# A planner's clock gets a duration for each kind of operation, and a bank's addition gets a due time

## The chip, the cores and the metric

The kernel runs on one core of one Trainium2 chip. The metric is the device time of one execution in microseconds (us). The engines are TensorE (PE, with its weight loads as PEld), VectorE (DVE), ScalarE (ACT), GpSimd (POOL) and SyncE (SP, which issues most DMAs).

## The reference

Three layers follow each other on 16384 tokens of 192 channels. The weights of the convolution are a softmax over its 7 taps, one set for each of 8 groups of channels.

```python
out = einsum('hk,bskhg->bshg', softmax(weight), windows_of_7(x))   # causal, per sequence of 4096
h = out @ w_in1;  g = relu(h) ** 2;            x2 = g @ w_out1     # 192 -> 2048 -> 192
h = x2 @ w_in2;   g = maximum(0.01 * h, h);    y  = g @ w_out2     # 192 -> 2048 -> 192
```

## The kernel before

The tokens are cut into 32 tiles of 512 (`TT`). For each tile and layer the 2048 hidden columns are done in 8 steps of 256 (two chunks of 128), which makes 512 steps `s` (`steps`). The first 64 steps do tiles 0 to 3 in both layers (tiles 0 and 1 as a pair that shares its weights). From step 64 on a round of 32 steps does two tiles: 8 steps each for layer 1, then 8 each for layer 2. There are 14 rounds, and during 13 of them DVE prepares the next two tiles. Numbers are kept as a high and a low part in fp32r, so each product is made of several matmuls. Two matmuls of 64 rows run side by side in the two halves of the array.

In each step PE makes `h` of step s (`g1`, `h` in the profile, psum tiles with 4 buffers) and, in three groups between the h products, the second product of step s-2 (`g2_one`, into three of the four banks o0m, o1m, o0r, o1r). ACT evaluates h (`act`, lines 567 and 569), makes the high parts `hi` (line 594) and in layer 1 the square of one chunk (line 576). DVE makes the other square (line 574, layer 1), the low parts `lo` (line 598) and their sum `both` (line 610), which PE needs two steps later. This order of a step on ACT and DVE is `chain` in `single`.

When a tile's 8 steps are done (the steps with s mod 8 = 1, called leaving steps here), its three banks are emptied by `evac_one`: ACT copies bank E (line 733, "e") and half of F (line 736, "f"), DVE adds F and E (line 739, "z", the bank's addition), and in the next step M (lines 742 and 743). The new product in the next bank can't start before line 739 has read it. What is left then lies in queues of pieces: `leave` (split of layer 1's result into the next operand x at lines 466 and 475, or for layer 2 the transpose to the output tile y at lines 753 and 758, followed by 4 stores each on SP at line 787), `prep` (the convolution of the next tiles on DVE: transposes at line 402, first tap at line 424, six more taps at line 426 for each of three passes, then the split into x, whose copies between partitions go by DMA at line 444) and `dec` (weights). The output tile y has one buffer: the next pair's transposes wait for the stores of the last one. The first pair of layer 2 is emptied by `evac` with transposes at lines 847 and 852 and 12 stores.

From step 48 (`THREE`) on, `single` plans DVE and ACT with a small clock of its own in ns, `clock`: before each DVE operation of the chain, `fill` puts pieces from the queues as long as `ends`, a trial run of the rest of the chain, stays within the due time `by`; a piece that is not due yet may delay it by 40 at most. A piece is a tuple with its step and its cost first; the convolution's pieces come from this line of `conv`:

```python
return acc, [((750 if k else 490), lambda k=k: tap(k)) for k in range(K)]
```

so 490 stands for the first tap and 750 for the later ones; transposes have 700, low parts of the split 690 and lines 742 and 743 together 1300.

Of the kernel before, what the change touches and what calls it, by code (L numbers as in the profile page):

```python
# [18 lines left out]
P = 128  # L19
TT = 512  # L20
STEP = 4100
PAIR = 215.6
STEP_ = 18 * PAIR
ON_A, ON_D, LATENCY = 545, 615, 70
DEBT = -4000
LAG = 2
AHEAD = 2
# [4 lines left out]
COVER = 2  # L32
# [33 lines left out]
def conv_moe_moe2_kernel(  # L66
# [11 lines left out]
    B, S, D = x.shape  # L78
# [252 lines left out]
    own = const.tile([P, 2, H], F32, name="own")  # L331
# [56 lines left out]
    at, end = slice(HALO - K + 1, HALO), slice(HT - K + 1, HT)  # L388
# [113 lines left out]
    now, made = [0], {}  # L502
# [38 lines left out]
    hps, gsp, hi, lo, ops = {}, {}, {}, {}, {}  # L541
# [21 lines left out]
    def act(u, f):  # L563

        g = gsp[u, f] = pg.tile([P, TT], F32, tag="g", name="g")
        if u[0] == 1:
            nc.scalar.activation(out=g, in_=hps.pop((u, f)), func=ACTF.Relu)  # L567
        else:
            nc.scalar.activation(out=g, in_=hps.pop((u, f)), func=ACTF.Prelu, alpha=0.01)  # L569

    def square(u, f, vector):
        g = gsp[u, f]
        if vector:
            nc.vector.tensor_mul(out=g, in0=g, in1=g)  # L574
        else:
            nc.scalar.activation(out=g, in_=g, func=ACTF.Square)  # L576
# [12 lines left out]
    def high(u, f, dma=False):  # L589
        a = hi[u, f] = spare_tile() if late_chunk(u, f) else ph.tile([P, TT], F32R, tag="hi", name="hi")  # L590
        if dma:
            nc.gpsimd.dma_start(out=a, in_=gsp[u, f])
        else:
            nc.scalar.copy(out=a, in_=gsp[u, f])  # L594

    def low(u, f):
        b = lo[u, f] = spare_tile() if late_chunk(u, f) else pl.tile([P, TT], F32R, tag="lo", name="lo")
        nc.vector.tensor_sub(out=b, in0=gsp.pop((u, f)), in1=f32(hi[u, f]))  # L598
# [104 lines left out]
    def turns_of(p):  # L703
        return ((0, 1, 2), (1, 2, 0)) if p % 2 == 0 else ((2, 1, 0), (0, 2, 1))
# [153 lines left out]
    with tc.manual_schedule():  # L858
# [77 lines left out]
        def decode_one():  # L936
            cost, fn = dec.popleft()[1:3]
            fn()
            budget[0] -= cost
            return cost  # L940
# [5 lines left out]
        prep, leave = deque(), deque()  # L946
# [70 lines left out]
        first = (1, 0)  # L1017
# [51 lines left out]
        chain = {"A": [deque() for _ in range(4)], "Z": [deque() for _ in range(4)]}  # L1069
# [49 lines left out]
        def needed(s, n):  # L1119

            while n > 0 and dec and dec[0][4] <= s:
                n -= decode_one()
            return n
# [19 lines left out]

        clock = {"D": 0, "A": 0}

        def on(engine, took, after=0):
            clock[engine] = max(clock[engine], after) + took
            return clock[engine] + LATENCY

        def ends(chain, extra, at):  # L1150

            now_, done = dict(clock), {}
            now_["D"] += extra
            for name, engine, took, needs in chain:
                start = max([now_[engine]] + [done.get(n, at.get(n, 0)) for n in needs])
                now_[engine] = start + took
                done[name] = now_[engine] + LATENCY
            return now_["D"]

        def fill(s, chain, at, by, scalar=0):  # L1160

            while True:
                best = None
                for q in (leave, prep, dec):
                    if not q or (q[0][3] and not q[0][3]()):
                        continue
                    cost = q[0][1]
                    if cost < 0 and not scalar:
                        continue
                    if cost > 0:  # L1170
                        end = ends(chain, cost, at)
                        if end > (by if q[0][0] <= s else min(by, ends(chain, 0, at) + 40)):
                            continue
                    if best is None or q[0][0] < best[0][0]:
                        best = q
                if best is None:
                    return
                if best is dec:
                    decode_one()
                    continue  # L1180
                z = best.popleft()
                z[2]()
                if z[1] < 0:
                    scalar -= 1
                    on("A", -z[1])
                else:
                    on("D", z[1])

        def single(s, begun, A, Z, leaving, then, alone):

            l, u = A[0][0], A[0]
            p = A[1] // 2
            at = {"h": begun + 5 * PAIR + 2 * (3 + COVER) * PAIR + 300}
            first = min(j for order in turns_of(p) for j, k in enumerate(order) if k == (1 if (u[1] % 2 == 0) else 2))
            by = begun + 2 * STEP_ + (5 + 3 * first + COVER * first + 2) * PAIR - 250
            names = ("actZ", "actA") if l == 1 else ("actA", "actZ")
            chain = [(names[0], "A", ON_A, ("h",)), (names[1], "A", ON_A, ("h",))]
            if l == 1:
                chain += [("sqZ", "D", ON_D, ("actZ",)), ("sqA", "A", ON_A, ())]
            chain += [("hiA", "A", ON_A, ("actA",)), ("hiZ", "A", ON_A, ("sqZ", "actZ"))]  # L1200
            chain += [("loA", "D", ON_D, ("hiA",)), ("loZ", "D", ON_D, ("hiZ",)), ("c", "D", ON_D, ("loZ",))]
            do = {
                "actA": lambda: act(*A), "actZ": lambda: act(*Z), "sqZ": lambda: square(*Z, True), "sqA": lambda: square(*A, False),
                "hiA": lambda: high(*A), "hiZ": lambda: high(*Z), "loA": lambda: low(*A), "loZ": lambda: low(*Z),
                "c": lambda: add_low(u, p),
            }
            if alone:
                early, other, add_rest = leaving
                at["E"], at["F"] = begun + STEP_ - 3 * PAIR + 300, begun + STEP_ + 300
                chain = [("e", "A", ON_A, ("E",)), chain[0], ("f", "A", ON_A, ("F",)), ("z", "D", ON_D, ("F", "e"))] + chain[1:]  # L1210
                do.update(e=early, f=other, z=add_rest)
            elif leaving:
                for fn in leaving:
                    fn()
                at["F"] = begun + STEP_ + 300
                chain = [("e", "A", ON_A, ("F",)), ("e2", "D", ON_D, ("F",)), ("s", "A", 2 * ON_A, ("F",)), ("z", "D", 2 * ON_D, ("s",))] + chain
            while chain:
                name, engine, took, needs = chain[0]
                if engine == "D":
                    fill(s, chain, at, by, 1 if name == "loA" else 0)  # L1220
                if name in do:
                    do[name]()
                at[name] = on(engine, took, max([at.get(n, 0) for n in needs] + [0]))
                chain = chain[1:]
            if alone:
                leave.append((s, 1300, then[0], None, None))
                then = then[1:]
            return then

        prep_next = 2  # L1230
        begun = 0
# [3 lines left out]
        for s in range(NS):  # L1235
            u, p = steps[s]
            l, t = u
            leaving, alone = [], False
            u2, p2 = steps[s - LAG] if s >= LAG else (None, 0)
            if s == NS - 1:  # L1240
                advance(going)
            elif s < LAG or u2 in in_pair:
# [4 lines left out]
                if s >= LAG:  # L1247
                    f = 2 * p2 + u2[1] % 2
# [3 lines left out]
                    z = g2(pair, f)  # L1252
# [3 lines left out]
                    if f == NF - 1:  # L1256
                        leaving, then = evac(pair)
                going = follows
            else:
                z = g2_one(u2, p2)  # L1260
# [6 lines left out]
                if p2 == NP - 1:  # L1267
                    alone = True
                    leaving, then = evac_one(u2)
# [6 lines left out]
            A, Z = (u, 2 * p), (u, 2 * p + 1)  # L1276
# [16 lines left out]
            if leaving:  # L1293
                while leave:
                    z = leave.popleft()
# [9 lines left out]
            if three:  # L1305
                begun += STEP_
                if s == THREE:
                    clock["D"] = clock["A"] = begun
                if late:
                    if late[0] not in hi:  # L1310
                        high(*late[0])
                    low(*late.pop())
                needed(s, 10000)
                then = single(s, begun, A, Z, leaving, then if leaving else (), alone)
                release()
                if leaving:
                    own = (2, u2[1]) if u2[0] == 1 else None
                    wait = LEAVE if u2[0] == 1 else LEAVE + 2
                    leave.extend((s + wait + 0.5 * n, c, fn, gate, own) for n, (c, fn, gate, own) in enumerate(
                        [z if len(z) == 4 else z + (None,) for z in then]  # L1320
                    ))
                continue
# [34 lines left out]
            if alone:  # L1357
                then[0]()
                then = then[1:]
# [3 lines left out]
            if leaving:  # L1363
                own = (2, u2[1]) if u2[0] == 1 else None
# [38 lines left out]
```

## Time and profile before

| | |
|---|---|
| median of 3 runs | 2066.9 us (2065.8 to 2067.23) |
| the profiled execution | 2066.62 us, its span 2064.9 us, granted clock 0.998 |
| PE busy | 2050.2 us, 99% of the span |
| DVE busy | 1697.2 us, 82% |
| ACT busy | 1465.3 us, 71% |
| line 598 (lo) on DVE | 1022 times, mean 690 ns |
| line 610 (both) on DVE | 463 times, mean 692 ns |
| line 426 (later taps) on DVE | 174 for acc_a, mean 746 ns |
| line 424 (first tap) on DVE | 29 for acc_a, mean 483 ns |

The span runs from the first to the last instruction of the profiled execution. An engine that is busy nearly all the time sets the end, so the places to look for are those where it waits, and for whom. In a timeline a row has start, duration, engine, line, operation, output and input, a count where equal ones follow each other, and in brackets the engine's idle time ahead of it and what ended it.

### The profile page before, as it was taken

Reading aid. Unit: us, or ns where it says so; the run is one execution under the profiler, and the core shown is the slowest. Engines: PE = TensorE matmul, PEld = TensorE weight load, DVE = VectorE, ACT = ScalarE, POOL = GpSimd, SP = SyncE. Lnnn points to the kernel's source line nnn. Section 1 sums busy time; section 2 is a strip of 40 time slices with the busy share of each in tenths; the row PEclk is TensorE's granted clock in tenths of the full one; section 3 lists DMA queues with packets and bytes.
Section 4 is the critical chain, followed back from the end, with each engine's and each line's share of the span. In section 5 each row is a group of like instructions: output and inputs, shape, how many; then the busy total and the mean of one; then the engine's idle time right before and its main releaser. Section 6 shows DMA issues by size and latency. Waiting matters only on the chain.

```text
span 2064.9 us, 46890 instructions
## 1 busy us (share of the span) xinstructions
PE 2050.2 (99%) x18592; PEld 1974.7 (96%) x18592; DVE 1697.2 (82%) x2651; ACT 1465.3 (71%) x2651; POOL 30.9 (1%) x82
## 2 busy tenths in 40 slices
PE   9999999999999999999999999999999999999998
PEld 6999999999999999999999999999999999999997
DVE  8988878888887887879878788887878878788674
ACT  7887667677676776767677676776767667676774
POOL 1000210000000000000000000000000000000000
PEclk9999999999999999999999999999999999999999
DMA  8631131121212112131121211212122121311110
GB/s 188 159 98 37 24 60 27 41 38 47 39 25 57 32 42 37 31 59 27 38 39 41 45 27 41 38 47 38 25 52 33 46 36 28 62 27 38 23 34 17
DMA packets 233397, 95.24 MB, mean 46 GB/s; under 512 B 203928, under 2 KB 219416, under 8 KB 233176
## 3 DMA queue, kind: packets, MB, share of 16 engines
q1 hardware_dynamic: 230008, 89.06, 21.9%
q0 software_dynamic: 1168, 2.75, 0.7%
q8 instruction: 145, 2.38, 0.5%
q14 instruction: 76, 0.62, 0.1%
q10 hardware_dynamic: 2000, 0.42, 0.1%
HBM read 25.19 MB, written 12.58 MB: 18 GB/s over the span
## 4 chain that ended last, share of the span: by engine, by line
PE 92%; DVE 3%; ACT 2%; DMA 1%; SPq 1%; issue 1%; DVEq 0%; ACTq 0%
PE h L535 45%; PE o1m L535 16%; PE o0r L535 15%; PE o0m L535 8%; PE o1r L535 8%; ACT hi L594 1%; DVE lo L598 1%; DMA lent<-in_moe_w_out_dram 0%; DMA out_dram<-y 0%; DVE acc_a L426 0%; DVE acc_b L426 0%; SPq L787 0%; ACT g L567 0%; DVE g L574 0%; DVE x L475 0%
## 5 line engine op out<-in xcount | busy, mean ns | idle before, releaser
L535 PE MATMUL h<-x,w 64*128 64x512 f32 x9216 | 1349.5, 376 | 0.9 <-ACT g L569 0.5
L535 PEld LDWEIGHTS h<-x,w 64*128 64x128 f32 x9216 | 1063.2, 186 | 8.5 <-ACT g L569 0.9
L598 DVE TENSOR_TENSOR lo<-g,hi 128x512 fp32r<-128x512 f32 x1022 | 668.4, 690 | 296.5 <-ACT hi L594 282.0
L594 ACT CAST hi<-g 128x512 fp32r<-128x512 f32 x1020 | 590.0, 620 | 62.6 <-DVE g L574 51.7
L535 PE MATMUL o1m<-hi,w 64*128 64x512 f32 x2044 | 621.5, 381 | 1.0 <-DVE ring L739 0.8
L535 PE MATMUL o0r<-hi,w 64*128 64x512 f32 x1948 | 589.5, 380 | 0.4 <-DVE ring L739 0.3
L569 ACT ACTIVATE g<-h 128x512 f32<-128x512 f32 x512 | 282.9, 595 | 316.0 <-PE h L535 315.2
L535 PE MATMUL o0r<-lo,w 64*128 64x512 f32 (+1 forms) x1022 | 382.1, 376 | 0.0
L535 PEld LDWEIGHTS o1m<-hi,w 64*128 64x128 f32 x2044 | 357.7, 185 | 25.5 <-DVE ring L739 3.3
L567 ACT ACTIVATE g<-h 128x512 f32<-128x512 f32 x512 | 281.9, 594 | 133.1 <-PE h L535 130.8
L535 PEld LDWEIGHTS o0r<-hi,w 64*128 64x128 f32 x1948 | 342.9, 185 | 21.6 <-DVE ring L739 3.5
L535 PE MATMUL o1m<-both,w 64*128 64x512 f32 x926 | 348.5, 376 | 2.5 <-DVE both L610 2.5
L610 DVE TENSOR_TENSOR both<-lo 128x512 fp32r<-128x512 f32 x463 | 320.5, 692 | 18.4 <-PE h L535 0.5
L535 PE MATMUL o0m<-hi,w 64*128 64x512 f32 x1088 | 324.5, 378 | 0.0
L535 PE MATMUL o1r<-hi,w 64*128 64x512 f32 x1052 | 318.7, 378 | 0.0
L535 PE MATMUL o0m<-lo,w 64*128 64x512 f32 x560 | 208.2, 376 | 0.6 <-DVE lo L598 0.6
L535 PE MATMUL o1r<-lo,w 64*128 64x512 f32 (+1 forms) x526 | 197.9, 376 | 0.0
L535 PEld LDWEIGHTS o0m<-hi,w 64*128 64x128 f32 x1088 | 191.9, 186 | 1.2
L535 PEld LDWEIGHTS o0r<-lo,w 64*128 64x128 f32 (+1 forms) x1022 | 186.7, 183 | 0.5
L535 PEld LDWEIGHTS o1r<-hi,w 64*128 64x128 f32 x1052 | 186.1, 186 | 1.0
L535 PEld LDWEIGHTS o1m<-both,w 64*128 64x128 f32 x926 | 172.2, 186 | 4.1 <-DVE both L610 3.4
L576 ACT ACTIVATE g<-g 128x512 f32<-128x512 f32 x269 | 169.5, 633 | 7.9
(134 smaller groups left out, 1315.8 us busy)
## 6 DMA issues: line engine op xcount, KB each, us to landing
x<-x SPq DMA_DIRECT2D x189, 256.0 KB
out_dram<-y SPq DMA_DIRECT2D x186, 64.0 KB
raw_a<-in_x_dram SPq DMA_DIRECT2D x127, 64.0 KB
raw_b<-in_x_dram SPq DMA_DIRECT2D x62, 64.0 KB
lent<-in_moe_w_out_dram SPq DMA_DIRECT2D x13, 256.0 KB
lent<-in_moe_w_in_dram SPq DMA_DIRECT2D x13, 192.0 KB
lent<-in_moe_w_in_dram SPq DMA_DIRECT2D x13, 128.0 KB
lent<-in_moe_w_out_dram SPq DMA_DIRECT2D x13, 128.0 KB
```

The costliest lines, as they stand in the source:

```text
L535: return nc.tensor.matmul(out=o.rearrange("p (b a) -> p b a", a=2), lhsT=w, rhs=z.rearrange("p (a b) -> p b a", a=2), start=begin, stop=end_,)
L567: nc.scalar.activation(out=g, in_=hps.pop((u, f)), func=ACTF.Relu)
L569: nc.scalar.activation(out=g, in_=hps.pop((u, f)), func=ACTF.Prelu, alpha=0.01)
L576: nc.scalar.activation(out=g, in_=g, func=ACTF.Square)
L594: nc.scalar.copy(out=a, in_=gsp[u, f])
L598: nc.vector.tensor_sub(out=b, in0=gsp.pop((u, f)), in1=f32(hi[u, f]))
L610: nc.vector.tensor_add(out=c, in0=f32(lo[u, 2 * p]), in1=f32(lo[u, 2 * p + 1]))
```

## The change

The step `PAIR` of PE goes from 215.6 to 216 ns, one duration for ACT and one for DVE becomes a table by kind of operation (`TOOK`), pieces get planned durations by their tag (`PIECE`), the delay until another engine sees a result becomes one for each engine, and `by` has a due time for the bank's addition `z` beside that for `both` (`c`). A piece is put only if neither of the two comes later than its due time (a piece not due yet: than 40 more). Output transposes of layer 2 get a gate: not before step s + 5 of the leaving step s.

```diff
-PAIR = 215.6
+PAIR = 216
-ON_A, ON_D, LATENCY = 545, 615, 70
+TOOK = {"act": 500, "sqA": 525, "hi": 525, "e": 485, "f": 485, "sqZ": 612, "lo": 612, "c": 612, "z": 710}
+PIECE = {750: 420, 490: 668, 700: 660, 690: 610, 1300: 1325}
+AFTER_PE, AFTER_A, AFTER_D = 280, 140, 125
+MARGIN = 60
...
-                done[name] = now_[engine] + LATENCY
-            return now_["D"]
+                done[name] = now_[engine] + seen[engine]
+            return {name: done[name] for name in done if name in ("z", "c")}
...
-                    cost = q[0][1]
+                    cost = PIECE.get(q[0][1], q[0][1])
...
-                        end = ends(chain, cost, at)
-                        if end > (by if q[0][0] <= s else min(by, ends(chain, 0, at) + 40)):
+                        now_, then = ends(chain, 0, at), ends(chain, cost, at)
+                        if any(then[n] > max(now_[n] + 40, by[n] if q[0][0] <= s else 0) for n in then):
                             continue
...
-                    on("D", z[1])
+                    on("D", PIECE.get(z[1], z[1]))
...
-            at = {"h": begun + 5 * PAIR + 2 * (3 + COVER) * PAIR + 300}
+            at = {"h": begun + (5 + 2 * (3 + COVER)) * PAIR + AFTER_PE}
...
-            by = begun + 2 * STEP_ + (5 + 3 * first + COVER * first + 2) * PAIR - 250
+            by = {"c": begun + 2 * STEP_ + (5 + 3 * first + COVER * first + 2) * PAIR - MARGIN, "z": begun + STEP_ + (8 + COVER) * PAIR - MARGIN}
...
                     wait = LEAVE if u2[0] == 1 else LEAVE + 2
-                    leave.extend((s + wait + 0.5 * n, c, fn, gate, own) for n, (c, fn, gate, own) in enumerate(
+                    later = None if u2[0] == 1 else lambda at=s + wait: now[0] >= at
+                    leave.extend((s + wait + 0.5 * n, c, fn, gate or later, own) for n, (c, fn, gate, own) in enumerate(
```

PE's order is the same before and after. DVE's order moves, with some casts on ACT and the DMAs that go with the moved pieces on SP. The lines of the changed kernel are three higher than those of the profile. The 13 rounds from step 64 to step 479 all have the order of the first one.

DVE in steps 97 and 98 (129 and 130 are the same), from the `both` of step 96 to that of step 98, before:

```order
L610 TENSOR_TENSOR both<-lo 128x512
L426 SCALAR_TENSOR_TENSOR acc_b<-xT_b,taps,acc_b 128x512 x2
L739 TENSOR_TENSOR ring<-o0r,ring 64x512
L574 TENSOR_TENSOR g<-g 128x512
L598 TENSOR_TENSOR lo<-g,hi 128x512 x2
L610 TENSOR_TENSOR both<-lo 128x512
L742 TENSOR_TENSOR ring<-o1r,ring 64x512
L743 TENSOR_TENSOR ring<-o1r,ring 64x512
L574 TENSOR_TENSOR g<-g 128x512
L598 TENSOR_TENSOR lo<-g,hi 128x512 x2
L610 TENSOR_TENSOR both<-lo 128x512
```

and now:

```order
L613 TENSOR_TENSOR both<-lo 128x512
L429 SCALAR_TENSOR_TENSOR acc_b<-xT_b,taps,acc_b 128x512
L742 TENSOR_TENSOR ring<-o0r,ring 64x512
L429 SCALAR_TENSOR_TENSOR acc_b<-xT_b,taps,acc_b 128x512 x2
L577 TENSOR_TENSOR g<-g 128x512
L601 TENSOR_TENSOR lo<-g,hi 128x512 x2
L613 TENSOR_TENSOR both<-lo 128x512
L745 TENSOR_TENSOR ring<-o1r,ring 64x512
L746 TENSOR_TENSOR ring<-o1r,ring 64x512
L577 TENSOR_TENSOR g<-g 128x512
L601 TENSOR_TENSOR lo<-g,hi 128x512 x2
L613 TENSOR_TENSOR both<-lo 128x512
```

One tap stands ahead of the bank's addition instead of two, and two stand between it and the square. In step 96 one more tap has come in behind the square. The six later taps of acc_b, which went up to step 105, are thus done by step 100.

DVE in steps 104 and 105 (136 and 137), from the `both` of step 103 to that of step 105, before:

```order
L610 TENSOR_TENSOR both<-lo 128x512
L426 SCALAR_TENSOR_TENSOR acc_b<-xT_b,taps,acc_b 128x512
L574 TENSOR_TENSOR g<-g 128x512
L598 TENSOR_TENSOR lo<-g,hi 128x512 x2
L610 TENSOR_TENSOR both<-lo 128x512
L426 SCALAR_TENSOR_TENSOR acc_b<-xT_b,taps,acc_b 128x512
L397 MEMSET xT_a 128x6
L402 STREAM_TRANSPOSE xT_a<-raw_a 128x512
L739 TENSOR_TENSOR ring<-o1m,ring 64x512
L574 TENSOR_TENSOR g<-g 128x512
L598 TENSOR_TENSOR lo<-g,hi 128x512 x2
L610 TENSOR_TENSOR both<-lo 128x512
```

and now:

```order
L613 TENSOR_TENSOR both<-lo 128x512
L429 SCALAR_TENSOR_TENSOR acc_a<-xT_a,taps,acc_a 128x512 x2
L577 TENSOR_TENSOR g<-g 128x512
L429 SCALAR_TENSOR_TENSOR acc_a<-xT_a,taps,acc_a 128x512
L601 TENSOR_TENSOR lo<-g,hi 128x512 x2
L613 TENSOR_TENSOR both<-lo 128x512
L429 SCALAR_TENSOR_TENSOR acc_a<-xT_a,taps,acc_a 128x512
L742 TENSOR_TENSOR ring<-o1m,ring 64x512
L577 TENSOR_TENSOR g<-g 128x512
L601 TENSOR_TENSOR lo<-g,hi 128x512 x2
L613 TENSOR_TENSOR both<-lo 128x512
```

The transpose of the next pass has gone to step 101, and its taps stand here: three in step 104 and one ahead of the bank's addition in step 105. In the steps between, the new order has two taps ahead of the square in step 100; in 101 a copy and the transpose (lines 401 and 402), the square and the first tap; in 102 and in 103 an output transpose and a tap ahead of the square, where before the output transposes stood in 100 and 101. In step 121 the bank's addition now comes first, where a part of the split and two taps stood ahead of it; in 119 and 120 there are three taps each instead of two and one. In step 113 two taps ahead of the bank's addition are gone too.

DVE in steps 53 to 55, where the first pair's output transposes (line 847, two of them, and line 852) stand now; before, they stood in steps 50, 51 and 52:

```order
L613 TENSOR_TENSOR both<-lo 128x512
L601 TENSOR_TENSOR lo<-g,hi 128x512 x2
L613 TENSOR_TENSOR both<-lo 128x512
L850 STREAM_TRANSPOSE y<-ring 128x512 x2
L601 TENSOR_TENSOR lo<-g,hi 128x512 x2
L613 TENSOR_TENSOR both<-lo 128x512
L855 STREAM_TRANSPOSE y<-ring 128x512
```

They have moved by three to four steps. The next output transpose moves from step 59 to step 62, and one tap goes from step 49, behind the emptying of the pair's banks, to step 48 ahead of it.

## Rows read from the trace of the kernel before

**Rows 1.** The page, first part: busy time, share of the span, instructions

```profile
PE 2050.2 (99%) x18592; PEld 1974.7 (96%) x18592; DVE 1697.2 (82%) x2651; ACT 1465.3 (71%) x2651; POOL 30.9 (1%) x82
```

**Rows 2.** Waits: engine, tile, line, waited for; us in total, times, longest

```profile
PEld o0r L535 <- DVE ring L739: 3.5, 13, 0.6
...
PEld o1m L535 <- DVE ring L739: 3.3, 12, 1.0
```

**Rows 3.** Timeline of PE in steps 129, 137, 145 and 153

```profile
551.79 0.67 PE L535 MATMUL h<-x,w 64*128 64x512 f32 x4
...
553.88 0.38 PE L535 MATMUL o0r<-hi,w 64*128 64x512 f32 x1
...
583.29 0.67 PE L535 MATMUL h<-x,w 64*128 64x512 f32 x4
...
585.34 0.38 PE L535 MATMUL o1m<-hi,w 64*128 64x512 f32 x1
...
614.75 0.67 PE L535 MATMUL h<-x,w 64*128 64x512 f32 x4
...
616.49 0.38 PE L535 MATMUL o0r<-hi,w 64*128 64x512 f32 x1
...
645.90 0.67 PE L535 MATMUL h<-x,w 64*128 64x512 f32 x4
...
647.87 0.38 PE L535 MATMUL o1m<-hi,w 64*128 64x512 f32 x1
```

**Rows 4.** Timeline of DVE, steps 128 to 130

```profile
547.05 0.69 DVE L574 TENSOR_TENSOR g<-g 128x512 f32<-128x512 f32 x1
...
549.62 0.69 DVE L610 TENSOR_TENSOR both<-lo 128x512 fp32r<-128x512 f32 x1
550.23 1.53 DVE L426 SCALAR_TENSOR_TENSOR acc_b<-xT_b,taps,acc_b 128x512 f32<-128x512 f32 x2
551.80 0.69 DVE L739 TENSOR_TENSOR ring<-o0r,ring 64x512 f32<-64x512 f32 x1
552.52 0.69 DVE L574 TENSOR_TENSOR g<-g 128x512 f32<-128x512 f32 x1
...
554.63 0.69 DVE L610 TENSOR_TENSOR both<-lo 128x512 fp32r<-128x512 f32 x1
...
558.93 0.69 DVE L610 TENSOR_TENSOR both<-lo 128x512 fp32r<-128x512 f32 x1
```

**Rows 5.** Timeline of PE: first use of the `both` of step 130

```profile
559.79 0.38 PE L535 MATMUL o1m<-both,w 64*128 64x512 f32 x1
```

**Rows 6.** Timeline of DVE, steps 131 to 137

```profile
560.51 1.29 DVE L598 TENSOR_TENSOR lo<-g,hi 128x512 fp32r<-128x512 f32 x2 [0.29 <-ACT hi L594]
561.83 0.69 DVE L610 TENSOR_TENSOR both<-lo 128x512 fp32r<-128x512 f32 x1
...
569.99 0.74 DVE L426 SCALAR_TENSOR_TENSOR acc_b<-xT_b,taps,acc_b 128x512 f32<-128x512 f32 x1
570.65 0.69 DVE L574 TENSOR_TENSOR g<-g 128x512 f32<-128x512 f32 x1
...
582.33 0.16 DVE L401 COPY xT_a<-xT_a 128x6 f32<-128x6 f32 x1
...
583.27 0.68 DVE L739 TENSOR_TENSOR ring<-o1m,ring 64x512 f32<-64x512 f32 x1
```

**Rows 7.** Timeline of SP's queue: the first pair's stores

```profile
239.61 33.07 SPq L787 DMA_DIRECT2D out_dram<-y  x12
```

**Rows 8.** Timeline of DVE, steps 54 and 59

```profile
252.55 1.53 DVE L426 SCALAR_TENSOR_TENSOR acc_a<-xT_a,taps,acc_a 128x512 f32<-128x512 f32 x2
...
277.63 0.71 DVE L753 STREAM_TRANSPOSE y<-ring 128x512 f32<-128x512 f32 x1 [5.24 <-DMA out_dram<-y]
```

**Rows 9.** Timeline of PE: first use of the `both` of steps 59 and 62

```profile
280.90 0.48 PE L535 MATMUL o1m<-both,w 64*128 64x512 f32 x1 [2.49 <-DVE both L610]
...
293.80 0.38 PE L535 MATMUL o1m<-both,w 64*128 64x512 f32 x1
```

More of the change, by code (lines that the diff above doesn't have):

```diff
@@ L1144, in conv_moe_moe2_kernel @@
         clock = {"D": 0, "A": 0}
+        seen = {"A": AFTER_A, "D": AFTER_D}
         def on(engine, took, after=0):
             clock[engine] = max(clock[engine], after) + took
-            return clock[engine] + LATENCY
+            return clock[engine] + seen[engine]
         def ends(chain, extra, at):
@@ L1184, in fill @@
                     scalar -= 1
-                    on("A", -z[1])
+                    on("A", TOOK["hi"])
                 else:
-                    on("D", z[1])
+                    on("D", PIECE.get(z[1], z[1]))
         def single(s, begun, A, Z, leaving, then, alone):
@@ L1192, in single @@
             p = A[1] // 2
-            at = {"h": begun + 5 * PAIR + 2 * (3 + COVER) * PAIR + 300}
+            at = {"h": begun + (5 + 2 * (3 + COVER)) * PAIR + AFTER_PE}
             first = min(j for order in turns_of(p) for j, k in enumerate(order) if k == (1 if (u[1] % 2 == 0) else 2))
-            by = begun + 2 * STEP_ + (5 + 3 * first + COVER * first + 2) * PAIR - 250
+            by = {"c": begun + 2 * STEP_ + (5 + 3 * first + COVER * first + 2) * PAIR - MARGIN, "z": begun + STEP_ + (8 + COVER) * PAIR - MARGIN}
             names = ("actZ", "actA") if l == 1 else ("actA", "actZ")
-            chain = [(names[0], "A", ON_A, ("h",)), (names[1], "A", ON_A, ("h",))]
+            chain = [(names[0], "A", "act", ("h",)), (names[1], "A", "act", ("h",))]
             if l == 1:
-                chain += [("sqZ", "D", ON_D, ("actZ",)), ("sqA", "A", ON_A, ())]
-            chain += [("hiA", "A", ON_A, ("actA",)), ("hiZ", "A", ON_A, ("sqZ", "actZ"))]
-            chain += [("loA", "D", ON_D, ("hiA",)), ("loZ", "D", ON_D, ("hiZ",)), ("c", "D", ON_D, ("loZ",))]
+                chain += [("sqZ", "D", "sqZ", ("actZ",)), ("sqA", "A", "sqA", ())]
+            chain += [("hiA", "A", "hi", ("actA",)), ("hiZ", "A", "hi", ("sqZ", "actZ"))]
+            chain += [("loA", "D", "lo", ("hiA",)), ("loZ", "D", "lo", ("hiZ",)), ("c", "D", "c", ("loZ",))]
             do = {
@@ L1208, in single @@
                 early, other, add_rest = leaving
-                at["E"], at["F"] = begun + STEP_ - 3 * PAIR + 300, begun + STEP_ + 300
-                chain = [("e", "A", ON_A, ("E",)), chain[0], ("f", "A", ON_A, ("F",)), ("z", "D", ON_D, ("F", "e"))] + chain[1:]
+                at["E"], at["F"] = begun + STEP_ - 3 * PAIR + AFTER_PE, begun + STEP_ + AFTER_PE
+                chain = [("e", "A", "e", ("E",)), chain[0], ("f", "A", "f", ("F",)), ("z", "D", "z", ("F", "e"))] + chain[1:]
                 do.update(e=early, f=other, z=add_rest)
@@ L1214, in single @@
                     fn()
-                at["F"] = begun + STEP_ + 300
-                chain = [("e", "A", ON_A, ("F",)), ("e2", "D", ON_D, ("F",)), ("s", "A", 2 * ON_A, ("F",)), ("z", "D", 2 * ON_D, ("s",))] + chain
+                at["F"] = begun + STEP_ + AFTER_PE
+                chain = [("e", "A", "e", ("F",)), ("e2", "D", "z", ("F",)), ("s", "A", "e", ("F",)), ("z", "D", "z", ("s",)), ("s", "A", "e", ("F",)), ("z", "D", "z", ("s",))] + chain
+            chain = [(n, e, TOOK[t], needs) for n, e, t, needs in chain]
             while chain:
```

## The prediction

> **What bounds the kernel now.** First I read the busy times: TensorE (PE) works 99% of the span, VectorE (DVE) 82%, ScalarE (ACT) 71% [rows 1]. PE's instructions stand in the same order before and after the change, so the time moves only by the idle time of PE that the change takes away or adds; a piece moved on DVE costs nothing until a bank's addition (line 739, Z below) or the addition of the two low parts (line 610, BOTH below) comes later than PE wants it. Second, the waits: from step 48 on PE's weight loads waited for Z in 25 leaving steps [rows 2]. Third, PE's timeline around Z. In a step where nothing is late, the stretch from the four h products to the second o0r two groups later lasts 616.49 - 614.75 = 1.74 us (the pair at 614) [rows 3]. The same stretch takes 2.09 at 551.79 (step 129), 2.05 at 583.29 (step 137) and 1.97 at 645.90 (step 153) [rows 3]. So a late Z costs 0.35, 0.31 and 0.23 us in the steps with s mod 32 = 1, 9 and 25, and nothing at 17. There are 13 such rounds of 32 steps, from step 64 to 479; after that no convolution fills DVE. Fourth, one stop by itself: at 272 us DVE waits 5.24 us for the stores of the output tile y [rows 8], and PE then waits 2.49 us for BOTH [rows 9].
>
> **The change, step by step.** Clocks, margins and durations only decide where DVE's pieces stand. What matters is one entry: the table gives 420 ns to pieces tagged 750, and that tag is the later taps of the convolution (line 426; the first tap, line 424, has the tag 490 and gets 668). Two taps in a row take 551.80 - 550.23 = 1.57 us to the next start, 0.785 each; a tap ahead of a square takes 570.65 - 569.99 = 0.66 [rows 4, 6]. So the new model packs taps about 0.3 us too tightly each. Working by start-to-start times from rows 4 and 6: BOTH to the next piece 0.61, tap to tap or to Z 0.785, tap to square 0.66, Z to the next 0.72, square to BOTH 2.11 (it goes over ACT's copy), low to BOTH 1.32, independent pieces 0.61.
>
> *Steps 128 and 129.* In step 128 a tap comes in behind the square: 547.05 + 0.61 + 0.66 + 1.32 = 549.64 for BOTH, against 549.62: hidden, DVE waited for ACT there. In step 129 the order is tap, Z, tap, tap, square instead of tap, tap, Z, square. Z starts at 549.64 + 0.61 + 0.785 = 551.03, 0.77 earlier than 551.80, so the 0.35 us go. But one tap more stands ahead of the square: 551.03 + 0.72 + 0.785 + 0.66 = 553.20 (before 552.52), and BOTH starts at 555.31 (before 554.63).
>
> *Step 130.* The group there is unchanged (two halves of the main addition, square, two low parts, BOTH), and it ran without a break: 558.93 - 554.63 = 4.30 [rows 4]. So BOTH starts at 559.61 and ends 0.69 later, at 560.30. PE used it at 559.79 [rows 5], and without the stop in step 129 it wants it 0.35 earlier, at 559.44. Before, there were 0.17 us to spare; now PE waits 0.86. When one half of the array waits, the halves take some 0.1 to get in step again. I take **0.96**; bounds 0 (should the wait not be hit) and 1.3 (0.86 and the whole loss of a late Z).
>
> *Steps 131 to 137.* Step 131 waits for ACT before its low parts (0.29 of idle, row 560.51) and so goes with PE again; BOTH is at 561.83 in the times of before. From there the new order is one unbroken chain. Step 132 with two taps: 0.61 + 0.785 + 0.66 + 2.11, BOTH at 566.0. Step 133: copy and transpose 0.94 (582.33 to 583.27), square, first tap, about 3.85 in all: 569.85. Steps 134 and 135, an output transpose and a tap each: 0.61 + 0.61 + 0.66 + 2.11 = 3.99 each: 577.83. Step 136 with three taps: 0.61 + 0.785 + 0.66 + 0.61 + 0.66 + 1.32 = 4.65: 582.48. Step 137: a tap, then Z at 583.87, against 583.27 [rows 6]. Z was already late there, so 0.60 more is lost in full: 0.91 instead of 0.31. Bounds 0.3 and 0.9 more, since seven steps are added up.
>
> *Steps 145 and 153.* No tap stands ahead of Z any more: at 153 the 0.23 us go, at 145 nothing was lost. The four pieces more in steps 151 and 152 lie in time that DVE spends waiting for ACT. One round: -0.35 + 0.96 + 0.60 - 0.23 = **+0.98 us**, 13 rounds **+12.7**.
>
> *The start.* The gate on output transposes takes away the stop at 278: -2.6 (2.49 and 0.1). But the two first transposes of the pair move from step 50 to 54, to where DVE now starts two taps at 252.55 [rows 8]. Twelve stores of y lasted from 239.61 [rows 7] to 277.63, when the next transpose could start [rows 8]: 38.0 us. Now they start at about 253.3 and end at 291.3. The next transpose, in step 62, waits for them; its BOTH then starts at 291.3 + 0.61 + 1.32 = 293.2 and ends at 293.9, while PE wants it at 293.80 - 2.6 = 291.2 [rows 9]. A new stop of 2.7 to 2.8. DVE leaves it about 1 us behind, which the first of the 13 rounds has no idle time to make up: +1.0 (0 to 1.5). One tap more ahead of the copy out of o1m at step 49: +0.8 (0 to 0.8, one tap). Together -2.6 + 2.8 + 1.0 + 0.8 = **+2.0**.
>
> *At nothing.* ACT's casts to x (line 466) move by one to five steps; ACT is 71% busy [rows 1] and their copies are due steps later. On SP, x copies and loads now stand ahead of the four stores of step 158, which is earlier. The eight stores begun in steps 134 and 135 take 2.76 each [rows 7], 22 us, to some 593, about when the next x copies are issued; those are used in step 144, over 10 us later. If that cover went, each us would cost 13. The last two output transposes move from step 507 to 510 and still end before the last chunk.
>
> The profiled execution took 2066.6 us (its span 2064.9 and 1.7 around it), 0.3 under the median of the runs. Sum: 2066.6 + 12.7 + 2.0 = 2081.3; I say **2081.4**.
>
> *A rule against the trace.* BOTH lasts 0.69, yet the next piece starts 0.61 after it [rows 4]. The Trainium skill, VectorE: DVE Perf Modes, section Terms, says of DRAIN that the next operation can't issue until the pipe is empty. By that rule pieces would not overlap, the tap more in step 129 would cost its full 0.75 instead of 0.66, and the sum would be about 1 us higher; the trace disagrees with it by 0.08 us a piece, and I go by the trace.
>
> **Rivals.** *Faster.* PE does not wait at 130 and 137, because the moved taps find room: then only the late Z go, 13 x (0.35 + 0.31 + 0.23) = 11.6, with +2.0 of the start: 2057. It decides whether BOTH of step 130 ends by 559.44. For it: that is what a due time on Z does, and DVE idles 18% of the span [rows 1]. Against: rows 4 show steps 128 to 130 without idle time, and 0.17 us to spare. *About the same.* Only one of the two new waits comes: with 130 alone a round makes -0.35 + 0.96 - 0.31 - 0.23 = +0.07, with 137 alone -0.35 + 0.60 - 0.23 = +0.02; with the start 2069. *Slower still.* The eight stores, now packed against the x copies, hold x back at step 144, or the chain of steps 132 to 137 makes BOTH late there too: 1 us more a round, 2094. Against: over 10 us of cover, and 0.8 us or more before each BOTH.
>
> **How the numbers follow.** Forecast 0.73 (its own range 2075 to 2088, from the bounds of steps 130 and 137), faster 0.10, about the same 0.10, slower still 0.07. The range 2068 to 2088 takes in the rival in the middle. A measurement of this kernel tells about 0.2%, 4.1 us, from no change: faster 0.10, same 0.10, slower 0.80.
>
> **What would show it.** Right: PE's waits for Z gone in steps 129 and 153, larger by 0.6 in 137; 13 waits of 0.8 to 1.1 for BOTH in step 130; the stop at 278 gone and one of 2.7 near 291, with DVE waiting some 8 us for the stores. Wrong: no wait for BOTH in step 130, or Z in step 137 not later than before.

## The result and the profile after

The changed kernel takes 2081.78 us (median of 4 runs, 2080.8 to 2082.83); the kernel before, run beside it, takes 2066.78 (4 runs, 2065.8 to 2067.23). The ratio is 1.0071, its 95% interval 1.0059 to 1.0083: slower by 15.0 us. The profiled execution of the changed kernel took 2082.83 us (span 2081.1, granted clock 0.997).

The page's busy line, after:

```profile
PE 2054.9 (99%) x18592; PEld 1969.5 (95%) x18592; DVE 1696.2 (82%) x2651; ACT 1467.7 (71%) x2651; POOL 34.1 (2%) x82
```

Against [rows 1] every engine has the same number of instructions and almost the same busy time; DVE even works 1 us less. Of the 16.2 us between the two spans, 11.5 are idle time of PE and 4.7 are longer busy time of PE. The busy line doesn't show where: it says 99% in both kernels. The waits do (engine, tile, line, waited for; us in total, times, longest):

```profile
PEld o1m L538 <- DVE ring L742: 10.4, 14, 1.0
...
PEld o1m L538 <- DVE both L613: 7.4, 14, 0.5
...
PEld o0m L538 <- DVE lo L601: 6.5, 13, 0.8
PE o1m L538 <- DVE ring L742: 6.1, 14, 0.6
...
PE o1r L538 <- DVE lo L601: 3.4, 1, 3.4
...
PE o1m L538 <- DVE both L613: 3.1, 13, 0.2
```

Of the two rows of [rows 2] the one for o0r is gone, the one for o1m has grown from 3.3 to 10.4 us, and two waits that hardly stood there before (3 times and once) now come 14 and 13 times: for BOTH, and for a low part in the other half of the array. One wait of 3.4 us comes once.

To place them, I compared the length of each of the 512 steps (from the last h product of one step to that of the next) in the two traces; the places below, and those of the experiments, are differences to the profiled execution of the kernel before. A late BOTH or Z shows up in the length of the step that uses it, one or two later:

| place | predicted | measured |
|---|---|---|
| Z of step 129 (s mod 32 = 1) | -0.35 | -0.35 |
| BOTH of step 130 | +0.96 | +1.07 |
| Z of step 137 | +0.60 | +0.57 |
| Z of step 153 | -0.23 | -0.23 |
| the 13 rounds, without the item marked * | +12.7 | +12.85 |
| stop at 278 us | -2.6 | -2.75 |
| stop near 291 us | +2.8 | +3.91 |
| first steps behind that stop * | +1.0 | +1.47 |
| one tap at steps 48 and 49 | +0.8 | +0.82 |
| all other steps | 0 | -0.1 |

Measured, this makes 16.2 for the two profiled executions (2082.83 - 2066.62); the medians differ by 15.0, since the profiled execution of the changed kernel was the longest of its four.

DVE's timeline in steps 128 to 130, after; it answers to [rows 4], all 5.1 us later:

```profile
552.70 0.74 DVE L429 SCALAR_TENSOR_TENSOR acc_b<-xT_b,taps,acc_b 128x512 f32<-128x512 f32 x1
...
554.75 0.69 DVE L613 TENSOR_TENSOR both<-lo 128x512 fp32r<-128x512 f32 x1
555.36 0.74 DVE L429 SCALAR_TENSOR_TENSOR acc_b<-xT_b,taps,acc_b 128x512 f32<-128x512 f32 x1
556.14 0.69 DVE L742 TENSOR_TENSOR ring<-o0r,ring 64x512 f32<-64x512 f32 x1
556.86 1.54 DVE L429 SCALAR_TENSOR_TENSOR acc_b<-xT_b,taps,acc_b 128x512 f32<-128x512 f32 x2
558.32 0.68 DVE L577 TENSOR_TENSOR g<-g 128x512 f32<-128x512 f32 x1
...
560.42 0.69 DVE L613 TENSOR_TENSOR both<-lo 128x512 fp32r<-128x512 f32 x1
...
564.73 0.69 DVE L613 TENSOR_TENSOR both<-lo 128x512 fp32r<-128x512 f32 x1
```

And PE, first at the place of [rows 3] (step 129), then where it uses the BOTH of step 130 [rows 5]:

```profile
556.84 0.67 PE L538 MATMUL h<-x,w 64*128 64x512 f32 x4
...
558.58 0.38 PE L538 MATMUL o0r<-hi,w 64*128 64x512 f32 x1
...
564.75 0.48 PE L538 MATMUL o0m<-lo,w 64*128 64x512 f32 x1
565.48 0.48 PE L538 MATMUL o1m<-both,w 64*128 64x512 f32 x1 [0.24 <-DVE both L613]
```

The stretch over Z now takes 558.58 - 556.84 = 1.74 us, as in a step where nothing is late. From Z on DVE runs without a break: BOTH at 560.42 and, one unbroken group of 4.31 later, at 564.73. It ends at 565.42, and PE starts 0.06 behind that. Nothing of it is idle time of DVE: DVE is the slower engine for these three steps.

The same at step 137 [rows 6]: DVE's BOTH of step 131 and its Z of step 137, and PE's first product into o1m behind it:

```profile
567.63 0.69 DVE L613 TENSOR_TENSOR both<-lo 128x512 fp32r<-128x512 f32 x1
...
588.85 0.74 DVE L429 SCALAR_TENSOR_TENSOR acc_a<-xT_a,taps,acc_a 128x512 f32<-128x512 f32 x1
589.63 0.68 DVE L742 TENSOR_TENSOR ring<-o1m,ring 64x512 f32<-64x512 f32 x1
```

```profile
589.51 0.39 PE L538 MATMUL o0r<-hi,w 64*128 64x512 f32 x1
590.37 0.48 PE L538 MATMUL o1m<-hi,w 64*128 64x512 f32 x1 [0.46 <-DVE ring L742]
```

Last the stop at the start, which answers to [rows 7, 8, 9]. SP's queue with the first pair's stores, DVE and PE:

```profile
253.99 32.97 SPq L790 DMA_DIRECT2D out_dram<-y  x12
```

```profile
292.33 0.71 DVE L756 STREAM_TRANSPOSE y<-ring 128x512 f32<-128x512 f32 x1 [7.84 <-DMA x<-x]
292.97 1.25 DVE L601 TENSOR_TENSOR lo<-g,hi 128x512 fp32r<-128x512 f32 x2
294.25 0.69 DVE L613 TENSOR_TENSOR both<-lo 128x512 fp32r<-128x512 f32 x1
```

```profile
290.46 0.38 PE L538 MATMUL o0r<-hi,w 64*128 64x512 f32 x1
294.27 0.48 PE L538 MATMUL o1r<-lo,w 64*128 64x512 f32 x1 [3.44 <-DVE lo L601]
```

DVE waits 7.84 us. The row names a copy x<-x, since a wait for several transfers is put down to the one that came last by the profile; but that copy's landing ran from 292.19 to 293.14, when DVE had gone on, and the last of the twelve stores landed at 291.95. So the wait is for the stores, as the prediction had it (some 8 us). DVE goes on 1 us later than the predicted 291.3; for 0.7 of it the stores began that much later than 253.3, with all of the kernel 0.7 us later there. PE however does not stand there for BOTH, as it did in [rows 9], but for a low part (line 601), which it wants earlier.

### The profile page after: what moved, and what is told of

The parts are those of the page before. It is cut to its first block, busy times and chain, and to the rows that moved or that the text cites. A ratio compares the mean times of both kernels' runs of the same rounds, so it can differ in the third digit from the quotient of the medians.

```text
span 2081.1 us, 46905 instructions
## 1 busy us (share of the span) xinstructions
PE 2054.9 (99%) x18592; PEld 1969.5 (95%) x18592; DVE 1696.2 (82%) x2651; ACT 1467.7 (71%) x2651; POOL 34.1 (2%) x82
## 3 DMA queue, kind: packets, MB, share of 16 engines
q0 software_dynamic: 1168, 2.75, 0.7%
## 4 chain that ended last, share of the span: by engine, by line
PE 79%; DVE 14%; ACT 3%; issue 2%; DMA 1%; SPq 1%; DVEq 0%; ACTq 0%
PE h L538 39%; PE o1m L538 14%; PE o0r L538 13%; PE o1r L538 7%; PE o0m L538 6%; DVE lo L601 4%; DVE acc_a L429 3%; ACT hi L597 2%; DVE both L613 2%; DVE g L577 2%; DVE ring L742 1%; SPq L790 0%; DVE y L756 0%; DVE y L761 0%; DVE xT_a L405 0%
## 5 line engine op out<-in xcount | busy, mean ns | idle before, releaser
L538 PEld LDWEIGHTS o1m<-hi,w 64*128 64x128 f32 x2044 | 358.0, 186 | 32.3 <-DVE ring L742 10.4
```

Source lines behind the costliest of these rows:

```text
L538: return nc.tensor.matmul(out=o.rearrange("p (b a) -> p b a", a=2), lhsT=w, rhs=z.rearrange("p (a b) -> p b a", a=2), start=begin, stop=end_,)
```

## The experiments

Each kernel is the changed one with one edit (E5 and E6 with two, E8 with three), except E3, which is the kernel before with one part of the change. "A round" is the 32 steps of two tiles, 13 times in the kernel. E1 to E4 ran beside a run of the kernel before of 2067.64 us, E5 to E7 beside a median of 2067.26 (9 runs), E8 beside 2067.28 (9 runs). E1 to E4 and E7 are one execution each, and executions of the kernel before differ by up to 4 us (2064.34 to 2068.28), so these five rest on the lengths of the steps, which in the rounds agree to some 0.1 us from one round to the next in most places.

**E1: later taps planned at what they take.**

```diff
-PIECE = {750: 420, 490: 668, 700: 660, 690: 610, 1300: 1325}
+PIECE = {750: 785, 490: 510, 700: 660, 690: 610, 1300: 1325}
```

> The change with one line other: a later tap is planned at 785 ns and the first at 510, as the trace before has them. If the two wrong entries make the new waits: no wait for BOTH in steps with s mod 32 = 2, Z on time in those with 1, 9 and 25, so each round is 0.89 us shorter than before the change (0.35 + 0.31 + 0.23), 11.6 in all; the stop at 278 stays away (-2.7), the one near 290 stays (+3.8, and about 1.5 for the half clock behind it): about 2057. If the due time itself or the tighter margin is what costs: step 130 still waits about 1 us for BOTH, and the time stays over 2072.

Measured: 2058.23 us, 9.4 under the kernel before and 23.6 under the changed one. By places: Z of step 129 -0.35, BOTH of step 130 +0.18, Z of step 137 -0.31 (in three rounds -0.11), Z of step 153 -0.23. The tap at steps 48 and 49 costs nothing any more, the stop near 291 stays (+4.29). So the model's two entries for taps decide the sign of the change. The 0.18 that is left had not been expected. DVE's timeline, E1:

```profile
549.81 0.69 DVE L613 TENSOR_TENSOR both<-lo 128x512 fp32r<-128x512 f32 x1
551.17 0.69 DVE L742 TENSOR_TENSOR ring<-o0r,ring 64x512 f32<-64x512 f32 x1 [0.66 <-ACT ring L739]
551.89 0.75 DVE L429 SCALAR_TENSOR_TENSOR acc_b<-xT_b,taps,acc_b 128x512 f32<-128x512 f32 x1
552.56 0.68 DVE L577 TENSOR_TENSOR g<-g 128x512 f32<-128x512 f32 x1
...
554.66 0.69 DVE L613 TENSOR_TENSOR both<-lo 128x512 fp32r<-128x512 f32 x1
```

Nothing stands ahead of Z, yet it starts 1.36 us after BOTH: it waits for ACT's copy of half F. In the changed kernel, with a tap ahead of it, it started 556.14 - 554.75 = 1.39 after BOTH. The tap ahead of Z was thus nearly free, and each tap behind it delays BOTH. E8 takes this up.

**E2: one tap less in the leaving steps.**

```diff
-        def fill(s, chain, at, by, scalar=0):
+        def fill(s, chain, at, by, scalar=0, most=99):
...
-            while True:
+            while most > 0:
+                most -= 1
...
-                    fill(s, chain, at, by, 1 if name == "loA" else 0)
+                    fill(s, chain, at, by, 1 if name == "loA" else 0, 1 if alone and l == 1 and name == "sqZ" else 0 if alone and l == 1 and name in ("loA", "loZ", "c") else 99)
```

> The change, but in layer 1's leaving steps only one piece may stand between the bank's addition and the square, and none behind it; the tap taken out of step 97 then stands in step 100, all else is the same. If DVE's chain from step 96 to 98 makes the wait in step 98 (130): BOTH comes 0.78 earlier, and of the 1.07 us that PE waits there 0.1 to 0.3 are left. If the chain of steps 100 to 105 (132 to 137) is without idle time, the third tap in step 100 makes Z of step 105 (137) about 0.5 later, and 0.57 lost there become 1.0 to 1.1: 2081.8 - 13 x 0.4 = 2076.5. If the wait in step 98 has another cause (the square's way over ACT in step 98 itself, or PE's order): no change there, 2088.

Measured: 2080.72 us. In the rounds it went as expected: the loss at step 130 falls from 1.07 to 0.29, that of step 137 rises from 0.57 to 1.02, since the tap comes back in step 132 and lengthens the chain up to 137. The rounds make +8.6 us instead of +12.85. The total missed by 4, more than half of it at the start: the step with the stop cost 5.24 instead of 3.91, since PE's clock fell before PE went on (last section), and the first 48 steps, the same instructions in the same order, took 0.9 more in this run. Two things follow: the wait at step 130 is made of taps between Z and the square, and a tap that is only pushed into the next packed step is paid there.

**E3: the gate alone, in the kernel before.**

```diff
-                    leave.extend((s + wait + 0.5 * n, c, fn, gate, own) for n, (c, fn, gate, own) in enumerate(
+                    later = None if u2[0] == 1 else lambda at=s + wait: now[0] >= at
+                    leave.extend((s + wait + 0.5 * n, c, fn, gate or later, own) for n, (c, fn, gate, own) in enumerate(
```

> The kernel before with only the gate on the output transposes. If the gate only moves the stop of the start: the 2.7 us at 278 go, and 12 stores that start 13 us later make a stop of some 3.8 us near 291, with up to 1.5 more for a lower clock behind it; the rounds, whose order changes by taps and transposes in steps 100 to 103 only, lose and gain nothing: 2066.8 + 1.1 to 2.6 = 2068 to 2069.5. If the later output transposes are what costs in the rounds (steps 100 to 105): Z of step 105 later than before, and 5 us or more above that.

Measured: 2067.72 us. No step of the rounds from step 96 on changed its length. The stop at 278 went (-2.75) and one at step 64 came (+4.23), +1.16 in the step after it. So the gate costs nothing in the rounds by itself, and at the start it moves the stop and makes it larger. The whole time hides this: the start was 2.1 us longer (steps 49 to 479), and the very last chunk 1.3 shorter, where the granted clock falls at a moment that differs from run to run (10.0 us ahead of the end in the kernel before, 6.4 in E3).

**E4: no due time for the bank's addition.**

```diff
-                        if any(then[n] > max(now_[n] + 40, by[n] if q[0][0] <= s else 0) for n in then):
+                        if any(then[n] > max(now_[n] + 40, by[n] if q[0][0] <= s else 0) for n in then if n == "c"):
```

> The change, but only BOTH has a due time, the bank's addition none. Three taps then stand ahead of it in step 97 (129), and in steps 96, 98, 100 to 105 and 121 nothing moves. If a tap planned at 420 ns is the cause: Z comes 0.8 later than before the change and PE loses 0.35 + 0.8 = 1.15 there; BOTH of the next step, as late as in the change, is then hidden behind that (0 instead of 1.07). A round differs from the change's by about +0.1: 2083. If the due time of the bank's addition is the cause: 2067 to 2070.

Measured: 2083.7 us. DVE's timeline, E4, at step 129:

```profile
554.80 2.32 DVE L429 SCALAR_TENSOR_TENSOR acc_b<-xT_b,taps,acc_b 128x512 f32<-128x512 f32 x3
557.15 0.69 DVE L742 TENSOR_TENSOR ring<-o0r,ring 64x512 f32<-64x512 f32 x1
```

Step 129 has three taps ahead of Z and loses 0.82 to the kernel before where the changed one gained 0.35; the wait at step 130 is gone, since PE has been held up already; steps 137 and 153 are as in the changed kernel. The due time does what it says at one of the four places, and moves the loss one step on. The gain at step 153 isn't its work: the tight packing has used the taps up before that.

**E5: taps as in E1, and the gate on single tiles only**, so that the first pair's transposes stand at steps 51 and 52.

```diff
-PIECE = {750: 420, 490: 668, 700: 660, 690: 610, 1300: 1325}
+PIECE = {750: 785, 490: 510, 700: 660, 690: 610, 1300: 1325}
...
-                    later = None if u2[0] == 1 else lambda at=s + wait: now[0] >= at
+                    later = None if u2[0] == 1 or not alone else lambda at=s + wait: now[0] >= at
```

> Later taps planned at 785 ns and first taps at 510, and the gate only on the output transposes of single tiles, so that the first pair's transposes stand at steps 51 and 52 and their stores are over well before the next transpose in step 62. Theory (the stop near 291 us comes from the pair's later stores, and the half clock behind it from that stop): no stop near 278 or 291, no stretch at the half level there, the rounds as with the taps at 785 and the gate on all (about -0.7 us a round), so 2058.2 less 4.3 less 1.2: about 2052.7, 14 us under the kernel before. Rival (the half clock after 293 us comes by itself): 2054. Rival (the stores only shift the stop to another step): about 2058.

Measured: 2053.35 us (median of 5, 2052.62 to 2054.01), ratio to before 0.9935 (0.9923 to 0.9948). No stop at 278 or 291, and no stretch at the lower clock there. The transpose of step 62 (start, DVE's timeline of E5) finds the stores done and follows BOTH without idle time:

```profile
282.47 0.69 DVE L613 TENSOR_TENSOR both<-lo 128x512 fp32r<-128x512 f32 x1
283.08 0.70 DVE L756 STREAM_TRANSPOSE y<-ring 128x512 f32<-128x512 f32 x1
```

**E6: only the two entries exchanged**, with the gate of E5.

```diff
-PIECE = {750: 420, 490: 668, 700: 660, 690: 610, 1300: 1325}
+PIECE = {750: 668, 490: 420, 700: 660, 690: 610, 1300: 1325}
```

> The table's two entries for taps exchanged (later taps 668 ns, first taps 420) and the gate only on single tiles. Theory (what costs time is the number of taps ahead of the square in the leaving steps, and 668 is enough to hold back the second): order Z, tap, square in steps 97 and 105 as with 785, so the same rounds; the tap ahead of the copy out of o1m at step 49 stays and costs 0.8: about 2053.5. Rival (668 is still too tight by 0.12 a tap, and taps elsewhere make BOTH late): 0.1 to 0.5 us a round more, 2055 to 2060.

Measured: 2054.61 us (median of 5, 2053.24 to 2055.5), ratio 0.9941 (0.9928 to 0.9955). Step by step the rounds are those of E5; step 50 costs 0.83 for the tap of step 49. So 668, though 0.12 under the 0.785 that a tap in a row takes, is enough: what matters is whether the plan lets a second tap in.

**E7: the changed kernel without the gate.**

```diff
-                    later = None if u2[0] == 1 else lambda at=s + wait: now[0] >= at
+                    later = None if True else lambda at=s + wait: now[0] >= at
```

> The changed kernel without the gate on output transposes. Theory: the wait for BOTH of step 130 is that of the changed kernel, 1.07 a round, since the gate doesn't touch steps 128 to 130; Z of step 137 comes 0.3 later than before instead of 0.6, since the output transposes stand where DVE is less packed; steps 129 and 153 as in the changed kernel: +0.8 a round, 10.3 in all. At the start no stop near 291, that at 278 is larger by 2 to 2.5 us, with a short half clock behind it (1.3) if a stop's length decides that, and the tap at step 49 costs 0.8: 2067 + 10.3 + 3.0 + 1.3: about 2081. Rival (the gate itself makes the loss of step 137 and the stop at 278 stays as it was): 2075.

Measured: 2083.35 us, 2 more than expected. The rounds: step 130 +1.06, step 137 +0.34, steps 129 and 153 as before, so 0.8 a round as expected; the gate's share in the loss of step 137 is 0.23 of 0.57, by the output transposes that it puts among the taps. The start was mis-sized: the stores began at 242.82 instead of 239.61 and DVE could go on at 281.17 instead of 277.63, 3.5 us later. PE, itself 0.6 later there, idled for 5.41 us:

```profile
284.44 0.79 PE L538 MATMUL o1m<-both,w 64*128 64x512 f32 x1 [5.41 <-DVE both L613]
```

That is 2.9 more than the 2.49 of [rows 9] (2 to 2.5 expected). By the lengths of the steps the stop grew by 4.45 and the step behind it by 1.24; the 2.8 beyond the idle time go with the half clock (1.3 expected).

**E8: E5 with nothing between Z and BOTH in layer 1's leaving steps.**

```diff
-                    fill(s, chain, at, by, 1 if name == "loA" else 0)
+                    fill(s, chain, at, by, 1 if name == "loA" else 0, 0 if alone and l == 1 and name in ("sqZ", "loA", "loZ", "c") else 99)
```

(`fill` has the argument `most` of E2.)

> The kernel of e5 with no piece at all between the bank's addition and the square, nor before the low parts and BOTH, in layer 1's leaving steps. Theory (the 0.19 us still lost at step 132 in e1, e5 and e6 comes from the one tap left ahead of the square, since the bank's addition now starts only after ACT's copy of half F): this loss goes in 13 rounds, 2.4 us less than 2053.35, so about 2051; steps 129, 137 and 153 stay as in e5. Rival (the 0.19 us is a change in how the halves of the array run, not DVE's lateness): it stays, 2053. Third way (the two taps pushed back make the bank's addition of step 153 late, where one tap now stands ahead of it): up to 0.2 a round back, 2053.

Measured: 2050.93 us (median of 5, 2049.82 to 2052.78), ratio 0.9922 (0.9908 to 0.9936), the fastest version here. The loss at step 130 is 0 in all rounds, the rest as in E5. DVE's timeline of E8 at the place of the last one of E1:

```profile
543.82 0.69 DVE L613 TENSOR_TENSOR both<-lo 128x512 fp32r<-128x512 f32 x1
545.18 0.69 DVE L742 TENSOR_TENSOR ring<-o0r,ring 64x512 f32<-64x512 f32 x1 [0.66 <-ACT ring L739]
545.90 0.69 DVE L577 TENSOR_TENSOR g<-g 128x512 f32<-128x512 f32 x1
547.12 1.29 DVE L601 TENSOR_TENSOR lo<-g,hi 128x512 fp32r<-128x512 f32 x2 [0.52 <-ACT hi L597]
548.44 0.69 DVE L613 TENSOR_TENSOR both<-lo 128x512 fp32r<-128x512 f32 x1
```

BOTH comes 548.44 - 543.82 = 4.62 after the last one, against 4.85 in E1. A tap in that place costs only 0.23, since without it DVE waits 0.52 for ACT; that 0.23 was the 0.18 to 0.19 a round.

## Why the prediction was right, and where it was not

**Which number matters.** The prediction said that one entry, 420 for later taps, decides the packing. E1 and E6 show it for that entry and its neighbour together: with these two changed and nothing else in the model, the rounds go from +12.85 to about -9.5 us. First taps at 510 (E5) and at 420 (E6) make the same rounds, which points to the entry for later taps; but no run changed it alone, or the first tap's 668. The other durations, the delays and the margins were not undone one by one, nor the due time for Z with the right entries. What each does alone, and which of them brings the -9.5, stays open.

**Steps 128 to 130.** Right in order and almost in size. In the times of before (PE's step 129 starts 556.84 - 551.79 = 5.05 later after) Z starts at 551.09, BOTH of 129 at 555.37 and BOTH of 130 at 559.68; the prediction had 551.03, 555.31 and 559.61. PE loses 1.07 and not 0.96: BOTH was 0.07 later, and 0.14 instead of the assumed 0.1 came on top of its lateness of 0.93. Both halves of the array wait at that place, one for BOTH, the other for a low part (14 and 13 waits in the rows of PEld above).

**Steps 131 to 137.** The chain from BOTH of step 131 to Z of step 137 takes 589.63 - 567.63 = 22.00 us, against 583.87 - 561.83 = 22.04 by the sum of start-to-start times. The loss is 0.57 for 0.60.

**Steps 145 and 153** went as said, and nothing showed at the stores or x copies; the rival with 1 us a round more did not come. The rival at 2057 has its condition met in E1, where the taps do find room: 2058.2.

**The start.** This is the mis-sized part: +2.0 predicted, +3.4 measured in steps 49 to 65. The step "its BOTH then starts ... while PE wants it at 293.80 - 2.6 = 291.2 ... a new stop of 2.7 to 2.8" failed: the stop was 3.91 by the lengths of the steps. The prediction took the first use of BOTH as the moment at which PE stops, from the stop at 278. But PE stopped after 290.46 for the low part of the same step, a group of products earlier, and idled 3.44 us. This explains only a part: BOTH ended at 294.25 + 0.69 = 294.94, and PE, by the lengths of the steps 2.04 us ahead of the kernel before, would have stopped for it at 293.80 - 2.04 = 291.76 and idled 3.18. Of the rest, 0.3 are the stores, which held DVE from 253.99 to 292.33, 38.3 us instead of 38.0. And 0.47 us of the 3.91 are no idle time; the stop at 278 has such a part too (2.75 - 2.49 = 0.26), and here the clock fell within the same step. The step "DVE leaves it about 1 us behind ... +1.0" failed too, in kind: the 1.47 us behind the stop are no wait. There PE's clock was at its lower level (last section), and DVE caught up meanwhile; the first round then lost 0.91 at its BOTH of step 66, a little less than the later ones.

**Sum and median.** From the profiled execution the sum was 1.5 us short (2081.3 against 2082.83), nearly all of it by these two terms. That the forecast lies 0.4 from the median is in part luck: the profiled execution of the changed kernel was 1.05 over its own median.

**The rule on DRAIN** (the Trainium skill, VectorE: DVE Perf Modes, Terms) fares as before: in the changed kernel the next piece starts 555.36 - 554.75 = 0.61 us after a BOTH that lasts 0.69, and two taps and the square behind them start 558.32 - 556.86 = 1.46 apart, less than the two taps last (1.54). The rows show that recorded times overlap; whether the pipe was empty they can't show.

## What to carry to other kernels

A planner that packs one engine to the edge of a due time is only as good as its shortest wrong duration: check each entry against the start-to-start times of the trace, by kind of neighbour, before looking at the rules around it. A due time on one wait pushes the work into the next step of the same engine, so read the slack of what follows (here 0.17 us ahead of the next BOTH) before expecting the wait to vanish. Where a buffer is refilled after stores, moving its first writer back moves the whole train of stores back with it.

## What the runs showed of the hardware

*The clock after a stop.* Windows of the trace (from and to in us, PE busy, PEld, DVE, ACT, POOL, then the granted clock, DMA share and GB/s): first the kernel before around its stop, then the changed kernel, then E7.

```profile
278.00:281.00 3.00, 0.51 (x6) 0.11 (x3) 2.97 (x6) 0.33 (x1) 0.00 (x0) 1.00 1.01 238
281.00:285.00 4.00, 4.00 (x38) 3.58 (x40) 2.19 (x4) 2.07 (x4) 0.80 (x3) 1.00 0.82 123
```

```profile
290.80:292.00 1.20, 0.04 (x1) 0.00 (x0) 0.00 (x0) 0.00 (x0) 0.00 (x0) 1.00 0.93 197
292.00:294.20 2.20, 0.00 (x0) 0.00 (x0) 1.87 (x3) 0.00 (x0) 0.00 (x0) 1.00 0.89 137
294.20:295.60 1.40, 1.32 (x12) 1.17 (x14) 1.36 (x4) 0.00 (x0) 0.00 (x0) 1.00 0.73 119
295.60:298.60 3.00, 3.00 (x18) 2.38 (x16) 2.83 (x7) 1.78 (x4) 1.24 (x3) 0.51 0.82 197
```

```profile
281.50:283.00 1.50, 0.00 (x0) 0.00 (x0) 1.50 (x4) 0.00 (x0) 0.00 (x0) 1.00 0.79 125
283.00:284.40 1.40, 0.00 (x0) 0.00 (x0) 1.37 (x4) 0.00 (x0) 0.00 (x0) 0.59 0.66 105
284.40:290.00 5.60, 5.56 (x26) 4.50 (x28) 2.00 (x4) 1.75 (x4) 0.79 (x3) 0.50 0.25 33
```

After the stop of 2.49 us [rows 9] PE went on at the full level (2.4 GHz). After the one of 3.44 it ran 1.4 us at the full level and then at the half level (1.2 GHz), 18 matmuls in 3.00 us, where the row of the kernel before has 38 in 4.00. After the one of 5.41 in E7 the clock had fallen before PE went on. E1, E2, E3 and E4, with the same stop near 291 (3.44 to 3.52), show the half level too, and E5, without the stop, does not. In E2 and E4 it began before PE went on, so that its cost stands in the step of the stop itself (5.24 and 5.25).

By the lengths of the steps, the stop of the kernel before cost 0.26 us more than PE's idle time. Those of the changed kernel, E1, E3 and E4 cost 1.8 to 1.9 more, and those of E2 and E7, where the half level lasted longer (in E2 the granted clock was 0.50 from 295 to 301 us), 3.2 and 3.0 more. So the half level added some 1.5 to 2.9 us to a stop; the prediction had no term for it. The Trainium skill (TensorE: Matmul & The Clock Gate, Part 1) says that the array's clock is gated by how busy the engine has been, and that the kernels measured for it had two levels only. The rows agree with both: the granted clock is 1.00 or 0.50, and 0.59 and 0.51 are stretches in which it changed.

*A floor under the bank's addition.* Z waits for ACT's copy of half F, so taking pieces from ahead of it helps only until 1.36 us after BOTH (E1, E8). The prediction did not foresee it: in the kernel before DVE reached Z of step 129 only after two taps [rows 4], so that this wait did not show there.
